# Linear attention into a mixture of experts: other banks for the first group's last tiles, and a later place for two operands of x

## The chip, the cores and the metric

The kernel runs on one core of a Trainium2 chip. The metric is the device time in microseconds (us), the median of several runs. The profile is of one execution. The core has a matrix engine (PE, with its weight loads shown apart as PEld), a vector engine (DVE), an activation engine (ACT), a general engine (POOL) and a queue that issues transfers (SP). Each works through its own instructions in the order in which the program wrote them. PE accumulates into PSUM, which has eight banks of 128 x 512 float32; DVE and ACT read a bank out again, and only then may PE start another accumulation there.

## The reference

Attention without softmax over pairs: features `exp(±(x w_phi - max|x w_phi|))`, a key-value product, and a division. Its output x (2304 tokens, 512 wide) goes through four experts with two layers each; every token takes every expert, weighted by a normalised probability.

```python
def phi(x):
    proj = np.einsum('bhsd,df->bhsf', x, w_phi)
    proj = proj - np.max(np.abs(proj), axis=-1, keepdims=True)
    return np.concatenate([np.exp(proj), np.exp(-proj)], axis=-1)
...
for e in range(E):
    h = np.maximum(x @ w1[e], 0.0)
    out += p[:, e:e + 1] * (h @ w2[e])
```

The shapes are q, k, v (4, 8, 576, 64), w_phi (64, 128), w1 (4, 512, 1024) and w2 (4, 1024, 512), all float32.

## The kernel before

**Precision.** A float32 product is made of three matmuls of rounded operands: each operand is split into a part `hi` and a rest `lo`, and `lo*hi`, `hi*lo` and `hi*hi` are summed in one bank (`terms`). So each operand costs an ACT copy (`hi`) and a subtraction on POOL or DVE (`lo`).

**Groups of tokens.** The first group (four token tiles of 128) runs through all 16 units of experts while the attention of later tokens still goes on (`first_units`). A unit is a quarter of an expert: 256 of its 1024 hidden features. Two more groups (eight and six token tiles) then run through the 16 units each by a scheme of seven products in place of eight (`strassen_unit`, units 16 to 47). The products accumulate in banks named A, B, C and D, and each unit's second layer follows in the next unit.

**A unit of the first group.** 24 first-layer matmuls (L570) fill two banks; ACT makes the relu's `h_hi` and DVE its `h_lo` (L557). Then, one unit late, four second-layer tiles of six matmuls each (`l2_tile`, L534) multiply h with w2, and for each tile DVE adds the bank, times a probability, to the output (L544, here called the tile's evacuation). "Tile 14.2" is below the third tile of unit 14. The four tiles of unit 15 stand inside unit 16, behind its first product.

**Banks.** The pools hold two banks for the first layer and for A and B (`ps_l1`), two for second-layer tiles (`ps_l2`), three for the attention and for C and D (`ps_att`), and one for the attention's key-value product, from unit 16 on for every third second-layer tile (`ps_kv`). In the first group the tiles take the two banks of `ps_l2` in turn, so that a tile waits for the evacuation of the tile two before it.

**What sets the order.** Everything is written out by a planner: pieces of work have a due key, and `tick()` moves a clock by a step and writes what is due. An attention pair has 16 keys; the last pair starts at key 240, `LAST` is 277, and the first group's clock steps by (277 - 85) / (16 x 16 x 0.88) = 0.85 for each of 16 ticks of a unit. Engines never leave that order, so an instruction that waits holds up all that is written behind it on its engine.

**Other work of the stretch.** The second group needs combinations of x: T1, T2, T3, B22 and T4, made by `x_ops`. B22 (ACT `hi`, POOL `lo`, L638 and L642) is used by the sixth product of unit 16, and T4 (DVE L657 and L658, ACT `hi`, DVE `lo` L642) by the seventh, which adds to bank D; B22 and T4 are due from the first tick of unit 16, at `XA_START` with a gap of `XA_GAP`. From unit 16 on the first-layer weights need sums, too: four DVE additions (L474 to L477, `ws`) on a raw tile that is loaded by SP (L450) into one of two raw buffers; the POOL subtractions L501 follow, and the last of those that reads the raw tile frees it for the next load.

```python
load("w1", n + 2, 1)
...
for _ in range(len(pend) if n == NU else min(i, 1, len(pend))):
    pend.pop(0)()
    tick()
```

Of the kernel before, what the change touches and what calls it, by code (L numbers as in the profile page):

```python
# [11 lines left out]
F32 = mybir.dt.float32  # L12
# [8 lines left out]
def kernel(  # L21
# [17 lines left out]
    P = 128  # L39
# [6 lines left out]
    DM = NP * P  # L46
    NTT = NT // P
    NPAIR = B * NP
# [5 lines left out]
    PER = 16  # L54
# [7 lines left out]
    COPY_ENG, COPY_ENG0 = "vvaaaa", "vaaaaa"  # L62
    LO_ENG, LO_ENG0, HI_ENG, HI_ENG0 = "vgg", "vgv", "vg", "ag"

    X_IN, X_GAP, XA_START, XA_GAP, XA_LATE = 4, 1, 0.5, 0.45, 3.7
    FETCH = (12, 28, 40, 46)
    W_WAIT = (5.5, 4.0, 0, 3.5)

# [6 lines left out]
    ps_l2 = ctx.enter_context(tc.tile_pool(name="ps_l2", bufs=2, space=PSUM))  # L75
    ps_att = ctx.enter_context(tc.tile_pool(name="ps_att", bufs=3, space=PSUM))
    ps_kv = ctx.enter_context(tc.tile_pool(name="ps_kv", bufs=1, space=PSUM))
# [15 lines left out]
    def terms(l, r):  # L93

        if len(l) == 1:
            return ((l[0], r[0]),)
        return ((l[1], r[0]), (l[0], r[1]), (l[0], r[0]))
# [4 lines left out]
    def later(key, fn):  # L102
        heapq.heappush(queue, (key, next(count), fn))

    def run_until(key):
        while queue and queue[0][0] <= key:
            heapq.heappop(queue)[2]()
# [318 lines left out]
            later(PER * i + o, functools.partial(fn, i, *args))  # L426
    FIRST = PER * (NP - 1) + 37
    LAST = PER * (NPAIR - 1) + 37
    LAST_IN = PER * (NPAIR - 1) + 16.1


# [3 lines left out]
    NU = NE * NFC // 2  # L435
    clock = Pair()
# [6 lines left out]
    def tick():  # L443
        clock.key += clock.step
        run_until(clock.key)
# [68 lines left out]
    def convert(kind, n, wait):  # L514
# [3 lines left out]
        if kind == "w1" and n >= NU:  # L518
            for o, fn in ((wait[0], s_sums), (wait[0] + 0.5, s_hi), (wait[1], s_lo)):
                later(max(clock.key, LAST + XA_LATE + 1) + o * clock.step, functools.partial(fn, n))  # L520
        else:
# [3 lines left out]
    def l2_tile(n, h, j, tile, o):  # L525

        e = (n % NU) * 2 // NFC
        if n >= NU and tile % 3 == 0:
            ps = ps_kv.tile([P, DM], F32, name="l2", tag="kv")
        else:  # L530
            ps = ps_l2.tile([P, DM], F32, name="l2", tag="l2")
        for f in range(2):
            for k, (l, r) in enumerate(terms(h, weights["w2", n])):
                nc.tensor.matmul(  # L534
                    ps, lhsT=l[:, f, j * P : (j + 1) * P], rhs=r[:, f, :],
                    start=(f == 0 and k == 0), stop=(f == 1 and k == 2),
                )
            if f == 0 and n < NU:
                tick()
        p = pr[:, tile, e : e + 1]  # L540
        if n % NU == 0:
            nc.vector.tensor_scalar_mul(o, ps, p)
        else:
            nc.vector.scalar_tensor_tensor(o, ps, p, o, op0=ALU.mult, op1=ALU.add)  # L544
        if n % NU == NU - 1:
            nc.sync.dma_start(out[tile * P : (tile + 1) * P, :], o)
# [28 lines left out]
    def first_units():  # L575
        pend = []
        for n in range(NU):
            load("w1", n + 2, W_WAIT[0])
            h_hi = hp_.tile([P, 2, 512], F32R, name="h_hi", tag="h_hi")
            h_lo = hp_.tile([P, 2, 512], F32R, name="h_lo", tag="h_lo")  # L580
            for f in range(2):
                for k in range(NP):
                    l1_part(n, f, k)
                    if k < NP - 1:
                        tick()
                ps = banks.pop((n, f))
                nc.scalar.activation(h_hi[:, f], ps, AF.Relu)  # L587
                relu_lo(h_lo[:, f], ps, h_hi[:, f])
                tick()
            l1_done(n, W_WAIT[2:])  # L590
            if n:
                load("w2", n + 1, W_WAIT[1])
            for fn in pend:
                fn()
                tick()
            if pend:
                l2_done(n - 1, W_WAIT[2:])
            pend = [
                functools.partial(l2_tile, n, (h_hi, h_lo), j, j, out0[:, j]) for j in range(N0)
            ]  # L600
        return pend
# [158 lines left out]
    def second_units(pend):  # L760
        xs, ops = xa, None
        for n in range(NU, 3 * NU):
# [21 lines left out]
            if n == NU + 6:  # L784
# [3 lines left out]
            pend = [  # L788
                functools.partial(
                    l2_tile, n, h[b], j, xs.first + b * nj + j, (out0 if b == 0 else out1[0])[:, j]  # L790
                )
                for b in (1, 0) for j in range(nj)
# [6 lines left out]
    with tc.manual_schedule():  # L799
# [38 lines left out]
        def to_early():  # L838
# [10 lines left out]
            for i, fn in enumerate(fns):  # L849
                later(LAST_IN + X_IN + X_GAP * i, fn)  # L850

# [5 lines left out]

        later(LAST_IN, to_early)
        later(LAST + XA_LATE, to_late)
        clock.key = FIRST  # L860
        clock.step = (LAST - FIRST) / (NU * (2 * NP + 2 * N0) * SPREAD)
        pend = first_units()
        clock.key = max(clock.key, LAST + XA_LATE)
        run_until(clock.key)
# [41 lines left out]
```

## Time and profile before

| what | value |
|---|---|
| median of 3 runs | 999.67 us (997.65 to 999.84) |
| the profiled execution | 999.65 us, span of its instructions 997.9 us |
| mean granted share of PE's clock | 0.99 |
| busy share: PE, DVE, POOL, ACT | 97%, 66%, 53%, 43% |
| where PE is not full | some slices between 350 and 430 us; the first slice |

The page cuts the span into 40 slices of 24.9 us and prints the busy share of each engine in tenths, and the granted PE clock as a share of 2.4 GHz. Below it the trace can be asked for waits (who held whom), for the instructions in order of time, and for busy times in chosen stretches. A row of the timeline has the start, the duration, the engine, the source line, the operation, its tiles and, in brackets, the idle time ahead of it with what ended it. A matmul's duration runs to its modelled end, so that in a full row of matmuls one starts before the one ahead has ended.

### The profile page before, as it was taken

To read this page: it belongs to the slowest core of one execution; us is meant where nothing else is said; L and a number is where in the kernel's file an instruction comes from. 1 tells how busy PE (TensorE), PEld (TensorE's weight loads), DVE (VectorE), ACT (ScalarE), POOL (GpSimd) and SP (SyncE) were. 2 spreads that over 40 slices of the span, in tenths; PEclk is the share of its full clock that TensorE was granted. 3 is DMA by queue.
4 is the path that set the end of the run, shared out by engine and by line. 5 is a ranking of instruction groups with operands and counts; after the bars stand their busy time and mean duration, and the time that the engine had idled before them with its cause. 6 is when DMAs were issued, how large, how long until landed. Compare 5 with 4: busy or idle time off the path is not lost. (4 is left out here: it accounts for less than half of the span.)

```text
span 997.9 us, 13544 instructions
## 1 busy us (share of the span) xinstructions
PE 967.1 (97%) x5031; PEld 835.0 (84%) x5031; DVE 657.6 (66%) x990; ACT 426.4 (43%) x768; POOL 524.3 (53%) x403
## 2 busy tenths in 40 slices
PE   7999999999999988899999999999989999999998
PEld 6888888888888876678888888888878888888887
DVE  4666656657566585666666666767976677676764
ACT  4666555555455543233333333343343334343441
POOL 2555556545455355364555544554565565655651
PEclk9999999999999998899999999999999999999999
DMA  6433434334333342113121111121122222212211
GB/s 151 129 85 82 116 92 114 94 105 121 104 102 88 109 121 76 63 64 95 43 75 59 52 59 43 43 64 63 43 96 92 67 64 64 85 48 80 64 43 64
DMA packets 70610, 80.37 MB, mean 81 GB/s; under 512 B 34161, under 2 KB 36081, under 8 KB 70545
## 3 DMA queue, kind: packets, MB, share of 16 engines
q1 hardware_dynamic: 70544, 79.51, 26.9%
q8 instruction: 40, 0.66, 0.3%
q14 instruction: 26, 0.20, 0.1%
HBM read 72.00 MB, written 7.49 MB: 80 GB/s over the span
## 5 line engine op out<-in xcount | busy, mean ns | idle before, releaser
L544 DVE SCALAR_TENSOR_TENSOR out<-l,pr,out 128x512 f32<-128x512 f32 x270 | 200.5, 747 | 115.9 <-PE l L534 115.1
L534 PE MATMUL l<-w2hi,h_lo 128*128 128x512 f32 x576 | 229.6, 399 | 12.4 <-DVE out L544 12.4
L534 PE MATMUL l<-w2lo,h_hi 128*128 128x512 f32 x576 | 227.8, 395 | 0.0
L534 PE MATMUL l<-w2hi,h_hi 128*128 128x512 f32 x576 | 227.6, 395 | 0.0
L534 PEld LDWEIGHTS l<-w2hi,h_lo 128*128 128x128 f32 x576 | 109.3, 190 | 33.5 <-DVE out L544 15.1
L501 POOL TENSOR_TENSOR w1lo<-wraw,w1hi 128x512 fp32r<-128x512 f32 x64 | 79.6, 1264 | 94.9 <-ACT w1hi L493 57.0
L534 PEld LDWEIGHTS l<-w2hi,h_hi 128*128 128x128 f32 x576 | 109.0, 189 | 24.3
L464 POOL TENSOR_TENSOR w2lo<-wraw,w2hi 128x1024 fp32r<-128x1024 f32 x48 | 115.7, 2410 | 24.1 <-ACT w2hi L458 20.5
L534 PEld LDWEIGHTS l<-w2lo,h_hi 128*128 128x128 f32 x576 | 109.3, 190 | 17.9
L702 POOL TENSOR_TENSOR c<-u,s 128x512 f32<-128x512 f32 (+1 forms) x32 | 37.4, 1169 | 94.9 <-DVE u L689 94.9
L692 ACT ACTIVATE h_hi<-c 128x512 fp32r<-128x512 f32 (+1 forms) x96 | 55.2, 579 | 69.2 <-DVE c L689 68.1
L251 PEld LDWEIGHTS kv<-v,e 128*128 128x128 f32 x640 | 77.6, 192 | 3.3
L501 POOL TENSOR_TENSOR s_lo<-ws,s_hi 128x768 fp32r<-128x768 f32 x32 | 59.1, 1846 | 35.0 <-ACT s_hi L493 35.0
L251 PE MATMUL kv<-v,e 128*128 128x66 f32 x640 | 76.1, 271 | 0.0
L718 ACT ACTIVATE c<-c 128x512 f32<-128x512 f32 (+1 forms) x32 | 18.5, 579 | 124.2 <-POOL c L702 124.2
L557 DVE SCALAR_TENSOR_TENSOR h_lo<-l,h_hi 128x512 fp32r<-128x512 f32 x32 | 22.1, 691 | 69.7 <-ACT h_hi L587 69.7
L201 DVE TENSOR_REDUCE m<-proj 128x4 f32<-128x512 f32 (+1 forms) x80 | 50.4, 630 | 15.2 <-PE proj L189 14.7
L458 ACT ACTIVATE w2hi<-wraw 128x1024 fp32r<-128x1024 f32 x48 | 50.5, 1053 | 20.8 <-PE l L534 19.2
L699 POOL TENSOR_TENSOR h_lo<-c,h_hi 128x512 fp32r<-128x512 f32 (+1 forms) x32 | 37.7, 1177 | 40.7 <-ACT h_hi L692 40.7
L229 POOL TENSOR_TENSOR elo<-e,ehi 128x640 fp32r<-128x640 f32 x24 | 37.5, 1578 | 38.6 <-ACT ehi L221 38.5
L203 DVE TENSOR_TENSOR d<-proj,m 128x512 f32<-128x512 f32 (+1 forms) x80 | 51.1, 638 | 4.4
L570 PE MATMUL l<-x_hi,w1lo 128*128 128x512 f32 x128 | 53.2, 416 | 0.0
(148 smaller groups left out, 2207.9 us busy)
## 6 DMA issues: line engine op xcount, KB each, us to landing
wraw<-in_w_dram SPq DMA_DIRECT2D x96, 512.0 KB
kq<-in_kq_dram SPq DMA_DIRECT2D x31, 256.0 KB
rb<-rec_d SPq DMA_DIRECT2D x32, 144.0 KB
out_dram<-out SPq DMA_DIRECT2D x18, 256.0 KB
v<-in_v_dram SPq DMA_DIRECT2D x32, 128.0 KB
xd<-rb SPq DMA_DIRECT2D x8, 288.0 KB
xr<-xd SPq DMA_DIRECT2D x2, 768.0 KB
kq<-in_kq_dram SPq DMA_DIRECT2D x32, 32.0 KB
```

The costliest lines, as they stand in the source:

```text
L201: nc.vector.tensor_reduce(m[:, :g], psv, axis=AX.X, op=ALU.max, apply_absolute_value=True)
L203: nc.vector.tensor_tensor(d[:, :n].rearrange("p (g f) -> p g f", f=NF), psv, m[:, :g].unsqueeze(2).to_broadcast([P, g, NF]), op=ALU.subtract,)
L229: engine.tensor_tensor(lo[sl], e[sl], parts[0][sl].bitcast(F32), op=ALU.subtract)
L251: nc.tensor.matmul(s.kv[:, n * KW : (n + 1) * KW], lhsT=e[:, e0 : e0 + NF], rhs=s.v[:, t, h * KW : (h + 1) * KW], start=(c == 0 and j == 0 ...
L458: nc.scalar.activation(hi, raw, AF.Copy)
L464: nc.gpsimd.tensor_tensor(lo, raw, hi.bitcast(F32), op=ALU.subtract)
L501: nc.gpsimd.tensor_tensor(dst, src, hi.bitcast(F32), op=ALU.subtract)
L534: nc.tensor.matmul(ps, lhsT=l[:, f, j * P : (j + 1) * P], rhs=r[:, f, :], start=(f == 0 and k == 0), stop=(f == 1 and k == 2),)
L544: nc.vector.scalar_tensor_tensor(o, ps, p, o, op0=ALU.mult, op1=ALU.add)
L570: nc.tensor.matmul(banks[n, f], lhsT=l[:, ksl], rhs=r[:, k, :], start=(k == 0 and j == 0), stop=(k == NP - 1 and j == 2),)
L692: nc.scalar.activation(h[b][0][:, f, :nt], src, AF.Relu)
L699: nc.gpsimd.tensor_tensor(dst, src, hi.bitcast(F32), op=ALU.subtract)
```

## The change

Three edits. `LAST_PS` (key 264) names a point behind the attention's last use of its banks. From there on a second-layer tile of the first group takes its bank by its place in the unit: the first from `ps_l2`, the second and fourth from `ps_att`, the third from `ps_kv`. By the planner's steps key 264 lies inside unit 13, so that it holds for tiles 12.2 and 12.3 and all tiles of units 13, 14 and 15, 14 in all. And `XA_START` goes from 0.5 to 4.5, so that B22 and T4 are due four ticks later in unit 16.

```diff
-    X_IN, X_GAP, XA_START, XA_GAP, XA_LATE = 4, 1, 0.5, 0.45, 3.7
+    X_IN, X_GAP, XA_START, XA_GAP, XA_LATE = 4, 1, 4.5, 0.45, 3.7
...
+    LAST_PS = PER * (NPAIR - 1) + 24
...
         if n >= NU and tile % 3 == 0:
             ps = ps_kv.tile([P, DM], F32, name="l2", tag="kv")
+        elif n < NU and clock.key > LAST_PS:
+
+            pool, tag = ((ps_l2, "l2"), (ps_att, "att"), (ps_kv, "kv"), (ps_att, "att"))[j]
+            ps = pool.tile([P, DM], F32, name="l2", tag=tag)
         else:
             ps = ps_l2.tile([P, DM], F32, name="l2", tag="l2")
```

PE's instructions keep their order; what they wait for changes. Here is the first matmul of tiles 14.0 to 14.3 and 15.0 to 15.3 on PE before (the number behind `l` is the tile's, and the bracket holds the engines whose semaphores it waits for):

```order
L534 MATMUL l_4181<-w2hi,h_lo 128x512 [waits DVE_49,Activation_49]
...
L534 MATMUL l_4200<-w2hi,h_lo 128x512 [waits DVE_49]
...
L534 MATMUL l_4216<-w2hi,h_lo 128x512 [waits DVE_49]
...
L534 MATMUL l_4224<-w2hi,h_lo 128x512 [waits DVE_49]
...
L534 MATMUL l_4253<-w2hi,h_lo 128x512 [waits DVE_49,Activation_49]
...
L534 MATMUL l_4269<-w2hi,h_lo 128x512 [waits DVE_49]
...
L534 MATMUL l_4285<-w2hi,h_lo 128x512 [waits DVE_49]
...
L534 MATMUL l_4297<-w2hi,h_lo 128x512 [waits DVE_49]
```

And the same eight tiles now:

```order
L539 MATMUL l_4181<-w2hi,h_lo 128x512 [waits Activation_49]
...
L539 MATMUL l_4200<-w2hi,h_lo 128x512
...
L539 MATMUL l_4216<-w2hi,h_lo 128x512 [waits DVE_49]
...
L539 MATMUL l_4224<-w2hi,h_lo 128x512
...
L539 MATMUL l_4249<-w2hi,h_lo 128x512 [waits Activation_49]
...
L539 MATMUL l_4260<-w2hi,h_lo 128x512
...
L539 MATMUL l_4273<-w2hi,h_lo 128x512 [waits DVE_49]
...
L539 MATMUL l_4289<-w2hi,h_lo 128x512
```

Every tile waited for DVE; now only the third tile of a unit, in the one bank of `ps_kv`, does so, for the evacuation of the third tile of the unit before.

DVE in unit 16 before, from the evacuation of tile 15.0 (`out` of `l_4253`) to the first reading of bank B:

```order
L544 SCALAR_TENSOR_TENSOR out_86<-l_4253,pr,out_86 128x512
L657 TENSOR_TENSOR T_4264<-x_hi,T_3988 128x512 x2
L658 TENSOR_TENSOR T_4264<-T_4264,x_lo 128x512 x2
L544 SCALAR_TENSOR_TENSOR out_86<-l_4269,pr,out_86 128x512
L642 TENSOR_TENSOR T4lo<-T_4264,T4hi 128x512 x2
L544 SCALAR_TENSOR_TENSOR out_86<-l_4285,pr,out_86 128x512
L544 SCALAR_TENSOR_TENSOR out_86<-l_4297,pr,out_86 128x512
L689 TENSOR_TENSOR u_4313<-s_4245,B 128x512
```

And now (`l_4249` to `l_4289` are the same four tiles of unit 15):

```order
L549 SCALAR_TENSOR_TENSOR out_86<-l_4249,pr,out_86 128x512
L549 SCALAR_TENSOR_TENSOR out_86<-l_4260,pr,out_86 128x512
L549 SCALAR_TENSOR_TENSOR out_86<-l_4273,pr,out_86 128x512
L662 TENSOR_TENSOR T_4284<-x_hi,T_3988 128x512 x2
L663 TENSOR_TENSOR T_4284<-T_4284,x_lo 128x512 x2
L549 SCALAR_TENSOR_TENSOR out_86<-l_4289,pr,out_86 128x512
L647 TENSOR_TENSOR T4lo<-T_4284,T4hi 128x512 x2
L694 TENSOR_TENSOR u_4313<-s_4245,B 128x512
```

The four operations of T4 stand behind the evacuations of 15.1 and 15.2, no longer ahead of them, and `T4lo` behind that of 15.3. On POOL the subtraction of B22 changes places with one of the w2 weights. Before:

```order
L501 TENSOR_TENSOR w1lo<-ws,w1hi 128x256
L501 TENSOR_TENSOR s_lo<-ws,s_hi 128x768
L642 TENSOR_TENSOR B22lo<-xr,B22hi 128x512 x2
L464 TENSOR_TENSOR w2lo<-wraw,w2hi 128x1024
L702 TENSOR_TENSOR c_4341<-u_4339,s_4322 128x512
```

Now:

```order
L502 TENSOR_TENSOR w1lo<-ws,w1hi 128x256
L502 TENSOR_TENSOR s_lo<-ws,s_hi 128x768
L465 TENSOR_TENSOR w2lo<-wraw,w2hi 128x1024
L647 TENSOR_TENSOR B22lo<-xr,B22hi 128x512 x2
L707 TENSOR_TENSOR c_4341<-u_4339,s_4322 128x512
```

`B22lo` now waits behind `w2lo`; nothing moves on ACT or SP.

## Rows read from the trace of the kernel before

**Rows 1.** The page: busy tenths and granted PE clock in 40 slices of the span

```profile
PE   7999999999999988899999999999989999999998
PEclk9999999999999998899999999999999999999999
```

**Rows 2.** Waits of PE, 340 to 430 us (engine line, waited for: total, times, longest)

```profile
PE l L534 <- DVE out L544: 12.4, 4, 4.7
PE A L740 <- ACT s L686: 1.2, 1, 1.2
```

**Rows 3.** Stretches: us, busy time and instructions of each engine, granted clock, DMA share, GB/s

```profile
core 0: us, PE busy (x) PEld busy (x) DVE busy (x) ACT busy (x) POOL busy (x), PEclk, DMA share, GB/s
361.10:364.50 3.40, 3.40 (x9) 2.66 (x8) 2.57 (x4) 1.26 (x2) 0.00 (x0) 0.50 0.00 0
...
405.50:412.20 6.70, 6.10 (x14) 4.79 (x15) 3.73 (x6) 0.55 (x1) 0.00 (x0) 0.50 0.54 187
...
430.00:600.00 170.00, 170.00 (x745) 139.43 (x745) 110.70 (x160) 61.10 (x103) 85.57 (x59) 1.00 0.20 62
```

**Rows 4.** Timeline of PE: the matmuls around the waits

```profile
357.36 0.39 PE L534 MATMUL l<-w2hi,h_hi 128*128 128x512 f32 x1
360.52 0.50 PE L534 MATMUL l<-w2hi,h_lo 128*128 128x512 f32 x1 [2.78 <-DVE out L544]
...
376.94 0.50 PE L534 MATMUL l<-w2hi,h_lo 128*128 128x512 f32 x1 [1.99 <-DVE out L544]
...
391.28 0.50 PE L534 MATMUL l<-w2hi,h_lo 128*128 128x512 f32 x1 [2.87 <-DVE out L544]
...
406.10 0.80 PE L534 MATMUL l<-w2hi,h_lo 128*128 128x512 f32 x1 [4.75 <-DVE out L544]
...
418.72 0.39 PE L740 MATMUL A<-x_hi,w1lo 128*128 128x512 f32 x1
```

**Rows 5.** Timeline of DVE ahead of the first wait

```profile
356.49 3.32 DVE L654 TENSOR_TENSOR T<-T,x_lo 128x512 f32<-128x512 f32 x2
359.73 0.74 DVE L544 SCALAR_TENSOR_TENSOR out<-l,pr,out 128x512 f32<-128x512 f32 x1
```

**Rows 6.** Timeline of DVE ahead of the other three waits

```profile
373.15 2.94 DVE L375 TENSOR_TENSOR rb<-nd,rb 64x576 f32<-64x576 f32 x2
376.13 1.41 DVE L544 SCALAR_TENSOR_TENSOR out<-l,pr,out 128x512 f32<-128x512 f32 x2
377.46 0.75 DVE L474 TENSOR_TENSOR ws<-wraw 128x256 f32<-128x256 f32 x1
...
386.97 1.53 DVE L474 TENSOR_TENSOR ws<-wraw 128x256 f32<-128x256 f32 x1
...
390.48 1.40 DVE L544 SCALAR_TENSOR_TENSOR out<-l,pr,out 128x512 f32<-128x512 f32 x2
...
399.34 2.69 DVE L657 TENSOR_TENSOR T<-x_hi,T 128x512 f32<-128x512 f32 x2
401.96 3.42 DVE L658 TENSOR_TENSOR T<-T,x_lo 128x512 f32<-128x512 f32 x2
...
405.97 1.28 DVE L642 TENSOR_TENSOR T4lo<-T,T4hi 128x512 fp32r<-128x512 f32 x2
```

**Rows 7.** Timeline of SP's queue: weight loads and the last pair's reciprocals

```profile
350.43 0.58 SPq L450 DMA_DIRECT2D wraw<-in_w_dram  x1
...
368.13 1.09 SPq L365 DMA_DIRECT2D rb<-rec_d  x2
...
379.95 0.37 SPq L450 DMA_DIRECT2D wraw<-in_w_dram  x1
```

**Rows 8.** Timeline of ACT: the rounding that waited for a weight load

```profile
355.14 1.06 ACT L458 ACTIVATE w1hi<-wraw 128x1024 fp32r<-128x1024 f32 x1 [0.48 <-DMA wraw<-in_w_dram]
```

**Rows 9.** Timeline of POOL in unit 16

```profile
398.50 2.99 POOL L642 TENSOR_TENSOR B22lo<-xr,B22hi 128x512 fp32r<-128x512 f32 x2 [5.15 <-ACT B22hi L638]
401.45 2.78 POOL L464 TENSOR_TENSOR w2lo<-wraw,w2hi 128x1024 fp32r<-128x1024 f32 x1
```

## The prediction

> **What bounds the kernel now.** I began with the page's slices [rows 1]. PE is full nearly everywhere, so a microsecond taken from it is a microsecond of the kernel, wherever nothing else becomes late. The reader is to see the three slices of 8 tenths between 349 and 424 us, and the two of them in which the clock reads 8: something there both stops and slows PE. The waits of that stretch [rows 2] say what: PE waited 12.4 us in four pieces, each time at a second-layer tile (L534) for an evacuation (L544), and 1.2 us once elsewhere. The timeline places the four at 360.52, 376.94, 391.28 and 406.10 us, with 2.78, 1.99, 2.87 and 4.75 us [rows 4]. By counting matmuls between them these are tiles 12.2, 13.3, 14.2 and 15.3, all of which the change gives another bank.
>
> Then the stretches behind the waits [rows 3]. Behind the first, 361.1 to 364.5 us ran at a granted clock of 0.50, that is the 1.2 GHz level; two more stretches of 3.4 us behind the second and third wait read the same, and behind the fourth 6.7 us. The wait of 1.2 us left the clock at 1.00. From 430 us on PE is full at 1.00 through 600 us [rows 3], so what is won before 430 us is kept: a matmul takes 170/745 = 0.228 us there, a tile of six 1.37 us.
>
> Last, why DVE was late. Ahead of the first wait stood two additions of T1 that took 3.32 us [rows 5]; ahead of the second the multiplication by the last reciprocals, 2.94 us; ahead of the third the four sums for unit 17's weights, from 386.97 to 390.48 us; ahead of the fourth T4, 2.69 + 3.42 us [rows 6]. DVE has a burst of other work each time and an evacuation behind it, and two banks give PE a lead of only two tiles.
>
> **The change part by part.**
>
> *More banks, with nothing else late.* From 357.36 + 0.23 = 357.59 us, where 12.1 has been issued [rows 4], to the first product of unit 17 at 418.72 us [rows 4] PE has 174 matmuls: tiles 12.2 and 12.3 (12), the first layer of units 14 and 15 (48), tiles of units 13, 14 and 15 (72), and seven products of unit 16 (42). At 0.228 us they take 39.7 us and end at 397.3 us. It took 61.1 us. So 21.4 us are to be had: 12.4 of waits, about 8.2 of half clock (half of three times 3.4 us and of the 6.10 us busy in the last stretch), and 0.8 of starting up.
>
> *Where the next wait lies.* The third tile of a unit reuses the one bank of `ps_kv`, so 15.2 waits for the evacuation of 14.2; the other tiles have a lead of six or more. Without a wait 15.2 is due 126 matmuls after 357.59, at 386.3 us. The evacuation of 14.2 is the third behind the sums of unit 17, and these need the raw weights. The chain: the multiplication by reciprocals began at 373.15 us, but its transfer was issued at 368.13 us [rows 7] and DVE was occupied until then. PE will be five us earlier here. I estimate that it starts 2 us earlier, the middle between its old start (0 us earlier) and some 4 us (its data there 1 us behind the issue). The evacuations and sums behind it keep their distances, so the load of unit 17's raw weights goes out at 379.95 - 2 = 378 us [rows 7]. The nearest row for its landing is the load issued at 350.43 us, for which ACT waited until 355.14 us, 4.7 us [rows 8]; there was more traffic then, so I take 4 to 4.7 us: 382 to 382.7. The four sums took 3.5 us up to the evacuation [rows 6], three evacuations of 0.7 us each (1.40 for two [rows 6]) follow: 387.6 to 388.3 us if the sums are as fast, 1 to 2 us more if POOL is at work beside all of them (the first took 1.53 us, where another of the same kind took 0.75 [rows 6]). So 15.2 starts at 387.6 to 390 us, a wait of 1.3 to 3.7 us. The ends are 0 (everything moves up by 4 us) and 5.4 us (nothing moves up, landing in 4.7 and sums of 5 us). I take 2.4 us, the mean of the second and third wait of before, whose mechanism this is.
>
> *The clock behind it.* A wait of 1.99 us cost 3.4 us of half clock [rows 3, 4]: 1.7 us. The ends are 0 (a wait of about 1.2 us, which cost none) and 3.1 (as behind the fourth).
>
> *T4 and B22 later.* T4's four operations took 6.1 us beside POOL's 2.99 + 2.78 us of B22 and w2 [rows 6, 9]; `T4lo`, two operations of the same size with POOL idle, took 1.28 [rows 6], so alone the four would take 2.6. They now start after the evacuation of 15.2. With 15.2 begun at 388.7 and done at 390.9 us (half clock), T4 runs from 391.6 to 394.2 or 397.7 us; the evacuation of 15.3 and `T4lo` bring 396.2 to 399.7. Behind them DVE must still read B, A and D (0.7 us each, as an evacuation) before the seventh product may add to D: 398.3 to 401.8 us. PE reaches that product at 390.9 + 2.2 + 5 x 1.37 = 399.9 us. A wait of 0 to 1.9 us; I take 0.3, since POOL's work starts earlier than DVE's here and part of it is over. This edit by itself costs nothing as long as the five products hide it; put at the old place T4 would stand ahead of the evacuation of 15.1, which only matters if the lead in banks is used up.
>
> The rows show two DVE operations held while POOL ran: the four of T4 needed 6.1 us beside POOL, but pairs of the same size 1.28 us alone. The Trainium skill (SBUF — State Buffer, Who interferes with whom) says that a DVE operation with two SBUF inputs and a POOL operation that reads SBUF block each other for a whole instruction, the first to issue winning. The trace agrees [rows 6, 9]; by the rule alone T4 would meet both B22lo and w2lo again and take 6.1 us, and the sum would be 1.6 us smaller.
>
> *B22lo behind w2lo on POOL.* They change places: `w2lo` ran 2.78 us behind `B22lo` [rows 9]. The sixth product needs `B22lo` at about 398.5 us. The raw w2 weights are one load behind unit 17's; if that load starts when the other has landed (382.7 us), its 4.7 us, a rounding of 1.06 us on ACT [rows 8], `w2lo` and then 2.99 us of `B22lo` end by 394.3 us. Nothing, with a bound of 0 to 1 us.
>
> *Queued behind the new waits.* Behind 15.2 on PE stands all of unit 16. The outputs of unit 15 leave SP as soon as evacuated, ahead of the next weight load, as before. The 1.2 us wait of unit 17 on ACT [rows 2] depends on DVE and POOL work behind the seventh product, and moves along with it.
>
> Sum: 21.4 - 2.4 - 1.7 - 0.3 = 17.0 us. The profiled execution took 999.65 us, its span 997.9, and the median of the runs is 999.67, so the two need no correction: 999.65 - 17.0 = 982.6 us.
>
> **The rivals.** *A, no wait is left that slows the clock.* The chain to 15.2 comes 2 us sooner, the wait is short and the clock stays at 1.00: 20 to 21.4 us won, 978.3 to 979.7, say 979. For it: six banks more than double the lead. Against it: `ps_kv` recycles every fourth tile, and DVE's sums for unit 17 wait for a load that PE's speed doesn't move.
>
> *B, DVE's backlog moves into unit 16.* 15.2 waits like the fourth of before (4.75 us, with 6.7 us of half clock, 3.1 us) and the seventh product waits its 1.9: 21.4 - 9.7 = 11.7 won, 988.0 us. For it: DVE's work is not reduced, only its order and PE's lead change. Against it: DVE has reserve where PE is full, as the 110.7 us busy of 170 us behind 430 us tell [rows 3].
>
> *C, the banks change nothing.* If the four waits came from DVE having no time at all, PE would wait later for the same work: within 0.2%. Against it: DVE is busy 65% of the stretch behind 430 us and keeps PE full there [rows 3].
>
> *D, slower: the clock.* PE might go from bank to bank with small waits at each, and the clock stay at the lower level. A matmul then takes 6.10/14 = 0.43 us in place of 0.228 us [rows 3], 0.2 us more; the 21.4 us are used up once 107 of the 174 matmuls run so, and all 174 would give 999.65 - 21.4 + 34.8 = 1013 us. Against it: every fall stood behind a wait of 2 us or more, and the products and tiles from 430 us on go through all eight banks at 1.00 [rows 3]. The Trainium skill (TensorE: Matmul & The Clock Gate, A second HAM failure mode: psum-queue depth-cycling) tells of a kernel that fell so, by cycling through banks; the stretch from 430 us does not agree with it.
>
> **How the numbers follow.** A measurement of this kernel can tell about 0.2% (2 us) from no change. The forecast, 980.5 to 985.5 us, gets 0.63; A 0.17; B 0.13 (985.5 to 990); C 0.03; D 0.04. So faster by over 0.2% is 0.93, the same 0.03, slower 0.04. The predicted time is 982.6 us. The range reaches to A's lower end and half into B, 978.5 to 988 us, and leaves out about 2 in 10.
>
> **What would show each step right or wrong.** The waits of PE for L544 in the stretch should fall from 12.4 us to one of 1.3 to 3.7 us, at tile 15.2 (third tile behind the first product of unit 16), with one stretch of 3.4 us at 0.50 behind it. The first product of unit 17 should begin near 401.7 us, before 418.72. DVE should show T4 behind three evacuations. No wait should stand at tiles of units 12 to 14, nor at the sixth product. A wait at tile 14.2, or two half-clock stretches, speaks for B; PE starting tiles at 1.00 throughout for A. The prediction is wrong in its core if PE's new wait is not for DVE, or if time is lost again behind 430 us.

## The result, and the profile after

| what | before | after |
|---|---|---|
| median of the runs on one chip | 998.97 us (997.65 to 999.84) | 984.26 us (982.8 to 984.88) |
| the profiled execution | 999.65 us, span 997.9 | 984.48 us, span 982.7 |
| mean granted share of PE's clock | 0.99 | 0.997 |

The ratio is 0.9852, with a 95% interval of 0.9835 to 0.9869: 14.7 us faster. The prediction was 982.6 us, with a range of 978.5 to 988.0.

The page's slices of PE and of its clock, after, answer to [rows 1]:

```profile
PE   7999999999999998999999999999989999999998
PEclk9999999999999999999999999999999999999999
```

Of the three slices of 8 tenths one is left, and no slice's clock reads 8 any more. The waits of PE from 340 to 430 us, which answer to [rows 2]:

```profile
PE l L539 <- DVE out L549: 2.7, 1, 2.7
PE A L745 <- ACT s L691: 1.0, 1, 1.0
PE l L539 <- POOL w2lo L465: 0.2, 1, 0.2
```

The four waits of 12.4 us have become one of 2.7 (all lines stand five further down than before: L539 is L534, L549 is L544, L745 is L740). PE's timeline tells where, and what follows; 402.29 us is the first product of unit 17, which stood at 418.72 us [rows 4]:

```profile
389.30 0.56 PE L539 MATMUL l<-w2hi,h_lo 128*128 128x512 f32 x1 [2.66 <-DVE out L549]
...
400.79 0.50 PE L745 MATMUL D<-T4hi,w1lo 128*128 128x512 f32 x1
...
402.29 0.40 PE L745 MATMUL A<-x_hi,w1lo 128*128 128x512 f32 x1
...
410.41 0.50 PE L745 MATMUL A<-x_hi,w1lo 128*128 128x512 f32 x1 [1.02 <-ACT s L691]
...
721.15 0.69 PE L745 MATMUL A<-x_hi,w1lo 128*128 128x384 f32 x1 [2.55 <-ACT s L691]
```

The wait at 389.30 is tile 15.2, the third behind unit 16's first product. Stretches of after (busy time and instructions of each engine, then the granted clock), to be read beside [rows 3]:

```profile
389.50:393.00 3.50, 3.50 (x9) 2.73 (x9) 2.69 (x5) 1.12 (x3) 3.50 (x3) 0.51 0.62 236
393.00:424.00 31.00, 29.98 (x130) 23.87 (x129) 24.55 (x31) 12.54 (x22) 16.55 (x13) 1.00 0.22 68
430.00:600.00 170.00, 170.00 (x745) 139.45 (x744) 110.27 (x160) 60.55 (x102) 85.37 (x57) 1.00 0.19 63
600.00:720.00 120.00, 118.60 (x523) 97.34 (x521) 88.98 (x125) 44.90 (x79) 64.59 (x46) 1.00 0.15 44
720.70:724.10 3.40, 2.95 (x9) 2.75 (x10) 1.97 (x4) 1.27 (x4) 3.40 (x2) 0.50 0.62 228
```

One stretch near 1.2 GHz stands behind the wait, and from 393 to 720 us the clock is at 2.4 GHz. The last row is new: before, the same wait of 2.56 us in unit 32 (at 737.67 us) left the clock at 1.00; here 3.4 us at 0.50 go with it.

DVE from the last reciprocals to the seventh product, after, beside [rows 6]:

```profile
372.61 2.52 DVE L375 TENSOR_TENSOR rb<-nd,rb 64x576 f32<-64x576 f32 x2 [2.19 <-DMA rb<-rec_d]
375.16 1.41 DVE L549 SCALAR_TENSOR_TENSOR out<-l,pr,out 128x512 f32<-128x512 f32 x2
...
377.62 0.95 DVE L478 TENSOR_TENSOR ws<-wraw,ws 128x256 f32<-128x256 f32 x1
378.50 0.74 DVE L549 SCALAR_TENSOR_TENSOR out<-l,pr,out 128x512 f32<-128x512 f32 x1
380.98 1.29 DVE L562 SCALAR_TENSOR_TENSOR h_lo<-l,h_hi 128x512 fp32r<-128x512 f32 x2 [1.74 <-ACT h_hi L592]
382.38 1.70 DVE L475 TENSOR_TENSOR ws<-wraw 128x256 f32<-128x256 f32 x1
...
387.19 4.03 DVE L549 SCALAR_TENSOR_TENSOR out<-l,pr,out 128x512 f32<-128x512 f32 x6
392.04 0.75 DVE L549 SCALAR_TENSOR_TENSOR out<-l,pr,out 128x512 f32<-128x512 f32 x1 [0.81 <-PE l L539]
392.71 3.17 DVE L662 TENSOR_TENSOR T<-x_hi,T 128x512 f32<-128x512 f32 x2
395.80 1.28 DVE L663 TENSOR_TENSOR T<-T,x_lo 128x512 f32<-128x512 f32 x2
...
397.67 1.28 DVE L647 TENSOR_TENSOR T4lo<-T,T4hi 128x512 fp32r<-128x512 f32 x2
```

The multiplication by the reciprocals (`rb`) now waits for its transfer; before, DVE came to it late. From there on DVE has few gaps: four sums for unit 16, evacuations, four sums for unit 17, six evacuations (the third is 14.2's, which lets 15.2 start), T4 and B, A, D. Its longest wait behind `rb`, 1.74 us, leads to ACT:

```profile
378.67 0.85 ACT L494 ACTIVATE s_hi<-ws 128x768 fp32r<-128x768 f32 x1 [1.31 <-DVE ws L478]
379.42 1.05 ACT L459 ACTIVATE w2hi<-wraw 128x1024 fp32r<-128x1024 f32 x1
380.37 1.06 ACT L592 ACTIVATE h_hi<-l 128x512 fp32r<-128x512 f32 x2
382.37 0.94 ACT L494 ACTIVATE w1hi<-wraw 128x512 fp32r<-128x512 f32 x2 [0.94 <-DMA wraw<-in_w_dram]
```

There `s_hi` waits for DVE's sums, and the relu stands behind it. So that wait, too, hangs on DVE's sums, which stand behind `rb`. POOL beside T4, after, to be read beside [rows 9]:

```profile
390.00 2.39 POOL L465 TENSOR_TENSOR w2lo<-wraw,w2hi 128x1024 fp32r<-128x1024 f32 x1
392.34 2.99 POOL L647 TENSOR_TENSOR B22lo<-xr,B22hi 128x512 fp32r<-128x512 f32 x2
```

### The profile page after: what moved, and what is told of

Same layout as the page of the kernel before. It is cut to its first block, busy times and chain, and to the rows that moved or that the text cites. A ratio compares the mean times of both kernels' runs of the same rounds, so it can differ in the third digit from the quotient of the medians.

```text
span 982.7 us, 13544 instructions
## 1 busy us (share of the span) xinstructions
PE 961.0 (98%) x5031; PEld 831.2 (85%) x5031; DVE 658.1 (67%) x990; ACT 425.9 (43%) x768; POOL 523.4 (53%) x403
## 5 line engine op out<-in xcount | busy, mean ns | idle before, releaser
L549 DVE SCALAR_TENSOR_TENSOR out<-l,pr,out 128x512 f32<-128x512 f32 x270 | 200.0, 747 | 109.3 <-PE l L539 108.4
L539 PE MATMUL l<-w2hi,h_lo 128*128 128x512 f32 x576 | 228.1, 396 | 2.7 <-DVE out L549 2.7
L539 PE MATMUL l<-w2lo,h_hi 128*128 128x512 f32 x576 | 227.1, 394 | 0.2 <-POOL w2lo L465 0.2
L539 PE MATMUL l<-w2hi,h_hi 128*128 128x512 f32 x576 | 226.0, 392 | 0.0
L539 PEld LDWEIGHTS l<-w2hi,h_hi 128*128 128x128 f32 x576 | 108.7, 189 | 23.8
L539 PEld LDWEIGHTS l<-w2hi,h_lo 128*128 128x128 f32 x576 | 108.7, 189 | 22.3 <-DVE out L549 3.8
L539 PEld LDWEIGHTS l<-w2lo,h_hi 128*128 128x128 f32 x576 | 108.6, 188 | 18.4 <-POOL w2lo L465 0.6
L201 DVE TENSOR_REDUCE m<-proj 128x4 f32<-128x512 f32 (+1 forms) x80 | 50.4, 630 | 14.2 <-PE proj L189 13.8
L459 ACT ACTIVATE w2hi<-wraw 128x1024 fp32r<-128x1024 f32 x48 | 50.5, 1052 | 14.2 <-PE l L539 13.5
L494 ACT ACTIVATE s_hi<-ws 128x768 fp32r<-128x768 f32 x32 | 27.1, 847 | 60.5 <-DVE ws L478 60.5
```

Of the source, the lines that this page charges most:

```text
L201: nc.vector.tensor_reduce(m[:, :g], psv, axis=AX.X, op=ALU.max, apply_absolute_value=True)
L459: nc.scalar.activation(hi, raw, AF.Copy)
L539: nc.tensor.matmul(ps, lhsT=l[:, f, j * P : (j + 1) * P], rhs=r[:, f, :], start=(f == 0 and k == 0), stop=(f == 1 and k == 2),)
```

## The experiments

**How they are compared.** The runs of one program differ by 2 to 8 us, and in the profiles much of that lies ahead of the change: the last matmul of tile 12.1 starts between 355.9 and 362.4 us in the fourteen profiles, where the kernels still do the same work. So I compare differences of starts in the timelines: from that matmul to the first product of unit 17 (**stretch**); from the start of `rb` to the same product; and from unit 17's next product in bank A (410.41 us above) to the last matmul (**tail**). These scatter too: over three profiles of one program the stretch by 0.95 us (after) and 2.3 us (before), `rb` to unit 17 by 0.15 and 2.1 us.

| kernel | stretch, us | `rb` issued to started | `rb` to unit 17 | tail | half clock in unit 32 |
|---|---|---|---|---|---|
| before, three profiles | 61.36, 59.09, 60.44 | 5.02 in the first | 45.57, 43.45, 45.17 | 566.66, 566.75, 566.45 | no, no, no |
| after, three profiles | 45.45, 45.43, 44.50 | 4.66, 4.84, 4.15 | 29.68, 29.57, 29.53 | 568.04, 566.52, 568.16 | yes, no, yes |
| banks only | 46.12 | 4.22 | 31.01 | 568.14 | yes |
| place only | 51.50 | | 35.61 | 566.57 | no |
| six banks in turn | 45.15 | 4.57 | 29.57 | 568.11 | yes |
| sums of unit 17 later | 44.79 | 4.44 | 29.58 | 567.99 | yes |
| no sums of unit 17 | 44.18 | 4.85 | 28.51 | 568.12 | yes |
| unit 15 on old banks | 45.88 | 4.80 | 29.68 | 568.02 | yes |
| T4 early, two profiles | 43.09, 45.63 | 4.31, 5.78 | 27.96, 28.63 | 566.52, 567.96 | no, yes |

**Banks only.** The later place is undone.

```diff
-    X_IN, X_GAP, XA_START, XA_GAP, XA_LATE = 4, 1, 4.5, 0.45, 3.7
+    X_IN, X_GAP, XA_START, XA_GAP, XA_LATE = 4, 1, 0.5, 0.45, 3.7
```

> The new banks alone; T4 and B22 are due at the first tick of unit 16 again, as before. Theory (the lead in banks is what pays): PE has six banks' lead, so T4's place ahead of two evacuations costs only what the seventh product of unit 16 then waits for DVE; the one wait at tile 15.2 stays at 2.7 us. I expect 0 to 2 us above the changed kernel, 984.3 to 986.3 us, and no wait over 1 us at 15.3. Rival (T4's later place pays, since the fourth wait was the longest): 4.75 us of wait and about 3 us of half clock come back, some 992 us.

Measured: 984.97 us, ratio 0.9862 (0.9844 to 0.988). Waits of PE, and T4 on DVE:

```profile
PE l L539 <- DVE out L549: 2.7, 1, 2.7
PE D L745 <- DVE u L694: 1.3, 1, 1.3
PE A L745 <- ACT s L691: 1.0, 1, 1.0
```

```profile
390.34 3.21 DVE L662 TENSOR_TENSOR T<-x_hi,T 128x512 f32<-128x512 f32 x2
393.47 3.48 DVE L663 TENSOR_TENSOR T<-T,x_lo 128x512 f32<-128x512 f32 x2
...
398.73 1.40 DVE L549 SCALAR_TENSOR_TENSOR out<-l,pr,out 128x512 f32<-128x512 f32 x2
```

The banks alone bring 13.8 us by the ratio. With T4 in its old place, beside both subtractions of POOL, its two pairs take 6.7 us in place of 4.45, and the seventh product waits 1.3 us. T4's second pair ends no later for that, 24.5 us behind the start of `rb` here and in after; what comes later are the readings of B and D, behind the two evacuations of 1.40 us that now stand behind `T4lo`.

**Place only.** The tiles keep the two old banks; only B22 and T4 come later.

```diff
-        elif n < NU and clock.key > LAST_PS:
+        elif n < 0:
```

> The later place of T4 and B22 alone; all tiles of the first group take the two banks of before. Theory: the first three waits of before stay (2.8, 2.0 and 2.9 us, each with 3.4 us at half clock), the fourth (4.75 us with 6.7 us at half clock) goes, since T4 no longer stands ahead of the evacuations of 15.1 and 15.2: 999 - 6.5 to 8 = 991 to 992.5 us. Rival (T4's place is most of the gain): 984 to 987 us. Rival (nothing at all without banks): 999 us.

Measured: 990.7 us, ratio 0.9926 (0.9907 to 0.9944). The waits at 12.2, 13.3 and 14.2 are as before, the fourth, of 4.75 us, is gone. Its waits, the stretches behind the first and second, and T4 on DVE, where POOL's last subtraction had ended at 400.33 us:

```profile
PE l L539 <- DVE out L549: 7.5, 3, 2.9
```

```profile
362.10:365.50 3.40, 3.40 (x10) 2.65 (x9) 2.19 (x4) 1.06 (x2) 0.00 (x0) 0.50 0.00 0
377.10:380.50 3.40, 3.40 (x15) 2.83 (x16) 3.37 (x6) 0.78 (x2) 1.85 (x3) 1.00 0.23 87
```

```profile
400.33 1.28 DVE L662 TENSOR_TENSOR T<-x_hi,T 128x512 f32<-128x512 f32 x2
401.54 1.29 DVE L663 TENSOR_TENSOR T<-T,x_lo 128x512 f32<-128x512 f32 x2
```

This part alone brings 7.4 us, so the two parts are not additive (by the ratios 13.8 + 7.4 against 14.8): each of them removes the fourth wait. And the wait of 1.99 us, behind which the clock fell in the first profile of before, left it at 2.4 GHz here; half of such a stretch, 1.7 us, is part of what this profile gained.

**Six banks in turn.** No second-layer tile comes back to its bank before six others, so that 15.2 need not wait for 14.2.

```diff
-            pool, tag = ((ps_l2, "l2"), (ps_att, "att"), (ps_kv, "kv"), (ps_att, "att"))[j]
+            pool, tag = ((ps_l2, "l2"), (ps_att, "att"), (ps_kv, "kv"), (ps_att, "att"), (ps_l2, "l2"), (ps_att, "att"))[(4 * n + j) % 6]
```

> As the changed kernel, but the 14 tiles go round six places (l2, att, kv, att, l2, att), so that each bank comes back after six tiles or more and 15.2 no longer waits for 14.2. If the wait at 15.2 (2.7 us with 3.4 us of half clock) is a loss by itself, it shrinks to about 1.2 us without half clock and the time falls by 3 us, to about 981.3 us. Rival (DVE's work is the bound there): PE arrives sooner at the sixth and seventh products of unit 16 and waits there for DVE or for ACT behind it, 2 to 3 us in all, and the time is that of the changed kernel within 1 us, 983.3 to 985.3 us.

Measured: 983.82 us, ratio 0.9854 (0.9836 to 0.9871). PE's timeline:

```profile
386.86 0.50 PE L539 MATMUL l<-w2hi,h_lo 128*128 128x512 f32 x1 [1.34 <-DVE out L549]
...
397.06 0.51 PE L745 MATMUL C<-B22hi,s_lo 128*128 128x512 f32 x1 [1.59 <-ACT s L691]
399.58 0.51 PE L745 MATMUL D<-T4hi,w1lo 128*128 128x512 f32 x1 [0.85 <-DVE u L694]
```

T4 on DVE, and the subtraction of B22 on POOL beside it:

```profile
390.68 2.89 DVE L662 TENSOR_TENSOR T<-x_hi,T 128x512 f32<-128x512 f32 x2
393.50 2.37 DVE L663 TENSOR_TENSOR T<-T,x_lo 128x512 f32<-128x512 f32 x2
```

```profile
391.26 3.46 POOL L647 TENSOR_TENSOR B22lo<-xr,B22hi 128x512 fp32r<-128x512 f32 x2
```

Tile 15.2 now waits for the evacuation of 14.0, the first behind the sums. The wait is halved and no half clock follows it, 1.3 + 1.7 us less, but the stretch is only 0.3 us shorter than the changed kernel's first profile. What was won comes back at the sixth and seventh product, and from `rb` to unit 17 it is 29.57 us, as after.

**Sums of unit 17 later.** The changed kernel, but the four sums of unit 17 are due 4.2 ticks later, behind the evacuations of 14.0 and 14.1, so that that of 14.2 is the first behind them.

```diff
-            for o, fn in ((wait[0], s_sums), (wait[0] + 0.5, s_hi), (wait[1], s_lo)):
+            late_ = 4.2 if n == NU + 1 else 0
+            for o, fn in ((wait[0] + late_, s_sums), (wait[0] + 0.5 + late_, s_hi), (wait[1] + late_, s_lo)):
```

> As the changed kernel, but the four sums for unit 17's weights are due some four ticks later, so that on DVE they stand behind the evacuations of 14.0 and 14.1. If these sums are what 15.2 waits for, its wait falls from 2.7 to about 1.3 us and no half clock follows it. If that is a loss by itself, 981.3 us; if DVE's work as a whole is the bound, the products of unit 16 wait instead (about 2 us at the sixth, 0.4 at the seventh) and the time is within 1 us of the changed kernel's.

Measured: 985.69 us, ratio 0.9875 (0.9853 to 0.9897). 15.2 waits 1.29 us, the sixth product 1.56, the seventh 0.86; `rb` to unit 17 is 29.58 us. Another way to shorten the wait at 15.2, and the same end. The median lies 1.4 us above that of after, outside the 1 us named; in the profile tile 12.1 came 2.95 us later than in after.

**No sums of unit 17.** The four DVE sums of that unit are left out and a constant, written by POOL, stands in their place.

```diff
+        if n == NU + 1:
+            nc.gpsimd.memset(s, 0.5)
+            weights["w1", n] = (raw, s)
+            return
```

> As the changed kernel, but the four DVE additions that make unit 17's weight sums are left out (POOL fills the tile with a constant; the output is wrong for unit 17's share). DVE is freed of some 5 us just ahead of the evacuations of unit 14. Both theories expect no wait at 15.2 and no half clock behind it. Theory (T4's chain, which starts only behind the evacuation of 15.2 and holds up ACT's copy of bank C, sets the sixth product): a wait of 1.5 to 2 us at the sixth product and 0.5 to 1 us at the seventh remain, so that the first product of unit 17 comes only 1 us sooner than in the changed kernel and the time is 983 to 984 us. Rival (the sums are the whole of what is left): 984.3 - 4.4 = 979.9 us.

Measured: 988.28 us, ratio 0.9871 (0.9843 to 0.9899), above the 983 to 984 us expected, with tile 12.1 5.5 us later than in the changed kernel's profile: in the attention PE's clock stood at 0.50 from 56.8 to 67.0 us. No wait is left at 15.2; PE waits 2.14 us at the sixth product and 0.87 at the seventh. On DVE:

```profile
394.14 3.79 DVE L666 TENSOR_TENSOR T<-x_hi,T 128x512 f32<-128x512 f32 x2
397.86 3.47 DVE L667 TENSOR_TENSOR T<-T,x_lo 128x512 f32<-128x512 f32 x2
```

4.8 us of DVE's work are gone (382.38 to 387.19 us in after), and the stretch is 1.3 us shorter than in the first profile of after, `rb` to unit 17 1.0 to 1.2 us shorter than in all three. T4, which now meets both POOL subtractions in full, takes 7.3 us in place of 4.45, and DVE waits for PE at three evacuations. So of the 4.8 us of the sums only some 1.1 us shows at unit 17.

**Unit 15 on old banks.** Unit 15's four tiles use the two banks of `ps_l2` in turn.

```diff
-        elif n < NU and clock.key > LAST_PS:
+        elif n < NU - 1 and clock.key > LAST_PS:
```

> As the changed kernel, but the four tiles of unit 15 take the two banks of before; units 12 to 14 keep the new ones. Theory (behind unit 14 it is DVE's work and T4's chain that bind, not banks): 15.2 waits for 15.0's evacuation as long as it does now for 14.2's, 2.5 us or somewhat more, 15.3 about 0.5 us more, and the time is that of the changed kernel within 1 us. Rival (every unit's share of the banks pays): the fourth wait comes back, 3 to 6 us, 987 to 990 us.

Measured: 990.03 us, ratio 0.9893 (0.9868 to 0.9918). That is where the rival put the time, but not by its mechanism: no wait of 3 to 6 us came back, and in the profile the clock stood at 0.50 from 72.8 to 83.0 us, in the attention, and tile 12.1 came 5.2 us later than in after, so that the median tells little. The stretch is 45.88 us, `rb` to unit 17 29.68, and the one wait for an evacuation is 2.69 us, at 15.1 for that of 14.0 and not at 15.2. By this one profile, and with T4 at its later place, unit 15's banks pay almost nothing; those of units 12 to 14 carry the gain.

**T4 early.** Six banks in turn, unit 17's sums later, and the first four operations of T4 due behind T3, in unit 15, where they no longer stand between the evacuations and the seventh product.

```diff
-            fns = [fn for k in ("t", "T2", "T1", "t3", "T3") for fn in xa_ops[k]]
+            fns = [fn for k in ("t", "T2", "T1", "t3", "T3", "t4") for fn in xa_ops[k]]
...
-        spread([fn for k in ("B22", "t4", "T4") for fn in xa_ops[k]], XA_START, XA_GAP)
+        spread([fn for k in ("B22", "T4") for fn in xa_ops[k]], XA_START, XA_GAP)
```

> The ring of six banks and the later sums together, and T4's four DVE operations written ahead of unit 16, among the other sums of x, so that only its rounding and its rest stay in unit 16. Theory (T4's chain sets the sixth product): the waits at 15.2 and at the sixth product go down to under 1 us each, no half clock falls in unit 16, and the first product of unit 17 comes some 2 us sooner: 982 to 983 us. Rival (DVE's work as a whole is the bound, wherever it stands): the same work ahead of unit 16 makes another tile wait, and the time stays at 984.3 us within 0.7.

> The changed kernel once more, for a direct comparison with the kernel beside it and for a second profile: 983.5 to 985 us; a wait of 2.6 to 2.7 us at 15.2 with half clock behind it. The wait of 2.55 us in unit 32, which the change doesn't touch, is followed by half clock in some profiles and not in others; if that belongs to the program it will be as in the first profile of the changed kernel (half clock), if it is chance it may be either.

Measured on one chip: 985.98 us against 986.67 for the changed kernel again, both above what was expected. In the profile of T4 early the waits came out as the theory said (none at 15.2, 0.57 us at the seventh product, no half clock), but a new one of 1.69 us stands at the first product of unit 16. The changed kernel's second profile is the more telling one: tile 15.2 waited just as long, and the clock did not fall. PE's timeline and the stretch behind the wait:

```profile
392.57 0.50 PE L539 MATMUL l<-w2hi,h_lo 128*128 128x512 f32 x1 [2.66 <-DVE out L549]
...
403.95 0.50 PE L745 MATMUL D<-T4hi,w1lo 128*128 128x512 f32 x1 [0.85 <-DVE u L694]
```

```profile
392.60:396.00 3.40, 3.40 (x15) 2.79 (x16) 3.40 (x5) 1.29 (x3) 3.40 (x3) 1.00 0.67 249
```

Its stretch is still 45.43 us: with full clock PE came earlier to the seventh product, and waited 0.85 us there. So in this place the half clock cost nothing by itself.

**Both again, with more runs.**

> The same program as the run with six banks, later sums and an earlier T4, beside a second timing of the changed kernel on one chip. From the profiles so far it is 2.35 us shorter than the changed kernel from the last matmul of tile 12.1 to the second product of unit 17 (51.22 against 53.57), and 1.5 us in the tail when unit 32's wait of about 2.55 us costs no clock. If the stretch is what differs and nothing ahead of it, its median is 1.5 to 4 us under the changed kernel's in the same call, about 981 to 983. If the early sums cost the attention what the stretch gains (a half-clock stretch near 57 us was seen in the run with later sums alone), the two medians lie within 1 us.

> The changed kernel itself, as the measure for the run beside it: 984 to 986 us. If the half clock behind the wait of 2.7 us at tile 15.2 is the rule, the profile shows it again near 390 us; if it is left to chance, it comes or doesn't, and the stretch from the last matmul of tile 12.1 to the second product of unit 17 stays at 53.5 us either way.

Measured on one chip: 982.95 us (980.73 to 984.82), ratio 0.9851 (0.983 to 0.9871), against 984.65 (983.05 to 985.15), ratio 0.9865 (0.9848 to 0.9882). On both chips T4 early lies below the changed kernel, by 0.7 and 1.7 us, and both times the scatter is larger than that: a better version is not shown. In the third profile of the changed kernel the half clock stood behind 15.2 again, and the stretch was 44.50 us. T4 early's second profile lost what the first had won, and tells why. `rb` and the first product of unit 16, first profile of T4 early:

```profile
373.85 2.52 DVE L375 TENSOR_TENSOR rb<-nd,rb 64x576 f32<-64x576 f32 x2 [1.85 <-DMA rb<-rec_d]
```

```profile
385.27 0.47 PE L746 MATMUL A<-x_hi,w1lo 128*128 128x512 f32 x1 [1.69 <-DVE h_lo L563]
```

and second:

```profile
373.95 2.91 DVE L375 TENSOR_TENSOR rb<-nd,rb 64x576 f32<-64x576 f32 x2 [3.30 <-DMA rb<-rec_d]
```

```profile
385.73 0.47 PE L746 MATMUL A<-x_hi,w1lo 128*128 128x512 f32 x1 [3.91 <-DVE h_lo L563]
```

The reciprocals' transfer took 4.31 us from its issue in the one and 5.78 in the other. PE was 1.8 us earlier in the second (tile 12.1 at 356.95, not 358.72), and still `rb` did not start earlier: PE's lead became a wait of 3.91 us, with half clock behind it.

**The kernel before, twice more.**

> The kernel before itself, a second profile. If the half clock behind a wait of 2 to 3 us is a matter of chance, the four waits of the stretch come again with 2.8, 2.0, 2.9 and 4.7 us, but not behind each of them stands a half-clock stretch of 3.4 us; and behind the wait of 2.55 us in unit 32, which had none in the first profile, there may be one (the time from the second product of unit 17 to the end is then 568.1 us in place of 566.6). If the rule is fixed by the program, both profiles are the same in this: half clock behind all four, none in unit 32.

> As the run beside it, a third profile of the kernel before: by chance the half clock falls differently again; by the program it is the same. The multiplication by the last reciprocals starts about 15.8 us behind the last matmul of tile 12.1 in either case, held by DVE's other work and not by its transfer.

Measured: 1000.03 and 998.47 us. The four waits came again (2.61, 1.98, 2.86, 4.75 and 2.45, 1.98, 2.86, 4.76 us). In the second profile the clock stayed at 1.00 behind the second of them; in the third it fell behind all four. In unit 32 it fell in neither. `rb` started 15.6 and 15.3 us behind tile 12.1's last matmul, right behind an evacuation, without a wait for its transfer.

## Why the prediction was right, and where it was not

**The mechanism.** Right for the waits: 12.4 us of waits at four tiles, of which the banks leave one, at 15.2, for the evacuation of 14.2; no wait at units 12 to 14; the first product of unit 17 at 402.29 us, where 401.7 was expected. Rival A (no wait left) and D (the clock stays low) are out by the trace, C by the time. Of B, DVE's backlog in unit 16, there is more than I gave it, below.

**The terms of the sum.** From 12.1's issue (356.84 + 0.23 us) to unit 17 it took 45.2 us, where 39.7 + 4.4 = 44.1 were predicted.

| term | predicted | in the profile of after |
|---|---|---|
| wait at 15.2 | 2.4 us | 2.66 us |
| half clock behind it | 1.7 us | 3.5 us at 0.51: 1.7 us |
| seventh product | 0.3 us | 0.1 us (0.85 in the second profile) |
| starting up and short waits | 0 | the rest, 45.2 - 39.7 - 4.5 = 1.0 us |

The last line is the term that I left out: short stops at the first product of unit 16 and at a tile that waited 0.2 us for `w2lo`.

**The tail, a miss.** I took it that from 430 us on nothing changes, from a row that ends at 600 us. From unit 17's next product in bank A the first profile of after needed 1.4 us more than that of before (568.04 against 566.66), because of the half clock behind the old wait in unit 32. The account of the profiled execution is then 982.6 + 1.1 (stretch) + 1.4 (tail) - 0.5 (tile 12.1 came at 356.84 in place of 357.36) = 984.6; it took 984.48. The median, 984.26, is 1.7 us above the forecast; only one of its four runs has a profile, so that this account holds for that run. The half clock in unit 32 stood in none of four profiles with the old banks and in eight of ten with the new ones, though the wait there is the same 2.5 to 2.6 us in all. The changed kernel itself ran with and without it. What decides it, these runs don't show.

**The way to 15.2, right by luck in part.** I let `rb` start 2 us earlier, with its data 1 us behind the issue. It started 0.54 us earlier (372.61, not 373.15): issued at 367.95 us, its data took 4.66. Raw weights did go out near 378 (378.64), and were read from 382.37 us on, 3.7 us later, not 4 to 4.7; the four sums took 4.8 us, not 3.5, with POOL's subtractions running beside them. The errors offset each other, and 15.2 started at 389.30, inside the 387.6 to 390 us named.

**The terms don't add.** This is the step of the reasoning that fell. I summed a wait, a slow stretch and a second wait on PE's path as if each could be taken away alone. Two kernels took away half of the wait at 15.2 and the half clock with it (six banks, later sums), the second profile of after the half clock alone, and from `rb` to unit 17 it stayed at 29.5 to 29.7 us; with the other two profiles of after and that of unit 15 on old banks that makes six with this figure. The end of the stretch is set by DVE's chain from `rb` through sums, evacuations and T4 to the reading of bank D; PE has 5 us more there than its matmuls need, and spends them at 15.2, or in half clock, or at the sixth and seventh product. T4's place moved the figure, in the old place to 31.0 us, early to 28.0 and 28.6, and so did leaving out the sums, to 28.5. So rival B's mechanism, DVE's work as the bound, held at a smaller price than its 988 us. The sum came out because its third term had been worked out behind the first two; what falls is the price of rival A, 979 us for a stretch without that wait. One slip of arithmetic beside it: by the chances given, the range leaves out about 0.14, not 2 in 10.

**T4 and POOL.** Predicted were 2.6 to 6.1 us for its four operations besides `T4lo`'s two; T4's two pairs took 3.17 + 1.28 us, the first beside `B22lo`, and `T4lo` 1.28. Where POOL was idle (place only), the first two pairs took 1.28 and 1.29 us; beside both subtractions (no sums) 3.79 and 3.47. The Trainium skill (SBUF — State Buffer, Who interferes with whom) says that a DVE operation with two SBUF inputs and a POOL operation that reads SBUF lock each other out for a whole instruction; these three rows agree with it.

**What fixes the end of T4.** DVE's queue alone does not. In the seven profiles with new banks and T4 in unit 16 behind its sums (after three times, banks only, six banks, sums later, unit 15 on old banks), T4's second pair ended 24.3 to 24.5 us behind the start of `rb`, though the first pair began anywhere from 17.9 to 20.7 us behind it. In each of them POOL ended `s_lo`, which needs DVE's sums, at 17.4 to 17.5 us and then had `w2lo` and `B22lo` to do, in one order or the other. In place only, where they did not meet, these took 2.4 and 2.55 us and T4's two pairs 2.6: one after the other 7.5 us, which from 17.45 us leads to 25.0, close to the 24.3 to 24.5 seen. So inside unit 16 an earlier T4 only meets more of POOL's subtractions. In T4 early the four operations stand ahead of `s_lo` and escape this; `T4lo`, which does not, took 3.51 us there in place of 1.28. Without the sums `s_lo` ended 0.9 us sooner, at 16.6 us, and T4 at 23.3. This is read from the traces; no kernel here moved POOL's subtractions, so what that would bring is not shown.

**The later place.** I costed it at nothing by itself, which understates it. With the old banks it brings 7.4 us, as it takes T4 from ahead of the fourth wait. Beside the new banks it takes away 1.3 us of wait at the seventh product and 1.3 us from `rb` to unit 17; the stretch, 0.7 us shorter, and the medians, 984.97 and 984.26, can't tell.

## What to carry to other kernels

Where PE waits for banks, count how many tiles it may run ahead of the reading engine's bursts, and give the tiles banks that others have stopped using; this took 9.7 of 12.4 us of waits and most of the half clock behind them. Then don't price the waits that are left one by one: follow the reading engine from the last thing that it truly waits for from outside (here a transfer of reciprocals), since a wait removed on PE ahead of that engine's chain comes back behind it. Ask, too, which other engine holds up that chain (here POOL's subtractions). To judge a change of 1 us, compare stretches between two fixed instructions, in more than one profile, not medians that scatter by several.

## What the runs showed of the hardware

- The same program, the same wait, and another clock: 2.65 to 2.66 us at tile 15.2 went with half clock (3.5 us at 0.51) in two profiles of the changed kernel and with 3.4 us at 1.00 in another; 1.98 to 1.99 us at 13.3 by half clock in two profiles of before and not in the third; 2.5 to 2.6 us in unit 32 by half clock in eight of fourteen profiles. In the attention, near 57 and 72 us, waits of 1.4 to 1.7 us went with half clock in four profiles, and others of 1.4 and one of 2.06 us did not. I had counted on 3.4 us of half clock behind every wait of 2 us and more, though the profile of before already had a wait of 2.56 us in unit 32 at full clock.
- Where the clock did fall in unit 32, the tail was 568.0 to 568.2 us, without it 566.5 to 566.8: 1.5 us, nothing in between.
- The transfer of the reciprocals took between 4.15 and 5.78 us from issue to first use where DVE waited for it, in seven kernels with the same issue. What makes it slower was not tried.
